# Batch 0 of an attention and MLP kernel: weight decoding moved ahead of the gate product in VectorE's queue, value loads moved ahead, raw down words in another pool

## The chip, the cores and the metric

One core of a Trainium2 chip runs the whole program. The metric is the device time in microseconds, the median of several runs; lower is better. TensorE is called PE, VectorE DVE, ScalarE ACT, GpSimd POOL and SyncE SP, as in the profile.

## The reference, cut to what matters

```python
def _attn_ref(q, k, v, p):              # batch 8, 8 heads, seq 576, head_dim 64, 32 packed queries
    p_packed = sm_attn(p, k, v)         # softmax attention of the 32 packed queries
    return sm_attn(q, p_packed, p_packed)

x = attn_out.transpose(0, 2, 1, 3).reshape(4608, 512)
g = x @ w_gate                          # [512, 1536]
x = (silu(g) * (x @ w_val)) @ w_out     # first MLP, d_ff 1536
h = x @ w_in                            # [512, 2048]
out = (h * cos(h)) @ w_out2             # second MLP, d_ff 2048
```

The weights come as 64-bit words, and the kernel makes 32-bit floats of them on the chip: this is the decoding that the change moves.

## The kernel before, in words

The order of the instructions on every engine is the order of the code (a manual schedule); each engine works through its own queue in order. Pools of buffers decide the rest: a new tile takes a free buffer, and its first writer waits until the last reader of the tile before is done. Pool "c" (`ct`) has 19 buffers, pool "w" (`wt`) 24, "m" (`mt`) 12, "s" (`ht`) 6, and PSUM has 8 banks.

Batches `b` 0 to 7 go through attention and the first MLP one after another; the second MLP follows for all tokens (L559 and L586). Inside a batch, `a_up` makes the 12 blocks `f` of 128 columns of the hidden layer, each in two halves `c` of 288 tokens: PE makes the gate `pg` and the value `pv`, ACT the silu, DVE the product `h` (L396), then ACT makes the rounded high part `g` (L77) and DVE the low part `g` (L78). This last pair is put off by one half: `flush_split` issues it in front of the next half's `h`. `a_down` multiplies by the down weights `wo` in 8 steps `n` (L438), and between these steps stands the attention of the next batch: `a_s1`, `a_t`, `a_pp`, `a_ppt`, `a_s2`, `a_wp`.

Batch 0 differs, for it also decodes the weights. There are 36 units of 128x512 words: 24 of gate and value weights (`wg`, two per block `f`) and 12 of down weights (`wo`, three per output block). A unit goes through three steps, and `u_step(k, n)` issues the next `n` units of step `k`:

- step 0, `u_load`: SP starts the DMA of the raw words (`raw`, 512 KB).
- step 1, `u_act`: ACT reads the words twice (L89 and L90) and leaves `dec` and a first version of the output.
- step 2, `u_dve`: DVE puts them together (L96 and L99). For a down unit, `flush_wo` then issues the split of the unit before into high (ACT L77) and low part (DVE L78).

Up to the loop over batches four units have been through step 2, six through step 1 and eight through step 0. From there `extra(0, f, c)` issues one of each at the end of each half. In block `f` PE first makes the first half of the sum of all four gate and value products (`u` = 0, L372), then `a_wp0(f + 1)` projects the decoded weights of the next block with the packed values (`wp`, L325: first with unit 2(f+1), then with unit 2(f+1)+1), then it makes the second half of the sums (`u` = 1). ACT copies the projection out of PSUM (`wpf`, L333) and then takes the silu of block `f`.

The value tiles `vt` of batch 1 are loaded by SP in `a_down(0)`, step 1; they take four buffers of pool "c", and `a_pp(1)` reads them in front of step 3. The raw words of the first eight down units are in pool "w", those of the last four in pool "c".

Of the kernel before, what the change touches and what calls it, by code (L numbers as in the profile page):

```python
# [19 lines left out]
B, H, S, D, NP = 8, 8, 576, 64, 32  # L20
NT, DM, DF1, DF2 = B * S, H * D, 1536, 2048
NF1, NF2, KD = DF1 // 128, DF2 // 128, DM // 128
NPAIR = H // 2
# [16 lines left out]
def attention_mlp_kernel(ctx: ExitStack, tc: tile.TileContext, qT, kT, vP, pP, wgv, w1o, w2, out):  # L40
# [15 lines left out]
    def ct(shape, dt, name):  # L56
        return sb.tile(shape, dt, tag="c", name=name, bufs=19)

    def mt(shape, dt, name):
        return sb.tile(shape, dt, tag="m", name=name, bufs=12)  # L60

    def ht(shape, dt, name):
        return sb.tile(shape, dt, tag="s", name=name, bufs=6)

    def bank(shape, name):
        return ps.tile(shape, F32, tag="b", name=name)
# [9 lines left out]
    def split(src, hi, lo, eng=DVE):  # L76
        ACT.activation(out=hi, in_=src, func=AF.Copy)  # L77
        eng.tensor_tensor(out=lo, in0=src, in1=hi.bitcast(F32), op=ALU.subtract)  # L78

    def raw_words(alloc, src, n):  # L80
        r = alloc([128, n, 2], U32, "raw")
        SP.dma_start(out=r, in_=src.bitcast(U32).rearrange("p (n t) -> p n t", t=2))
        return r
# [26 lines left out]
    def load_p(b):  # L110
        SP.dma_start(out=pt[b % 2], in_=pP[b])

    def load_k(b, j):
        kt[b, j] = mt([128, S], F32, "kt")
        SP.dma_start(out=kt[b, j], in_=kT[b, j])
# [5 lines left out]
    def load_v(b, j):  # L121
        vt[b, j] = ct([128, NC, 128], F32, "vt")
        SP.dma_start(out=vt[b, j], in_=vP[b, j])
# [132 lines left out]
    def u_load(n):  # L256
        if n >= len(units):
            return
        kind, a, i = units[n]
        d_raw[n] = raw_words(  # L260
            wt if 2 * NF1 <= n < 2 * NF1 + 8 else ct, wgv[a, :, 512 * i:512 * i + 512] if kind == "g" else w1o[a, i], 512
        )

    def u_act(n):
# [32 lines left out]
    def u_step(k, n):  # L297
        for _ in range(n):
            (u_load, u_act, u_dve)[k](u_next[k])
            u_next[k] += 1  # L300
# [3 lines left out]
    def w2_load(i):  # L304
        if i < 4 * NF2:
            w2_raw[i] = raw_words(mt, w2[i // 2, :, 256 * (i % 2):256 * (i % 2) + 256], 256)

    def w2_decode(i):
        w_ = ht([128, 256], F32, "w2f")
        t_ = ht([128, 256], F32, "w2t")  # L310
        decode_a(w2_raw[i], t_, w_)
        decode_b(w2_raw.pop(i), t_, w_)
        w2_out[i] = w_

    def w2_store(i):
        if i in w2_out:
            SP.dma_start(out=w2s[i // 2, :, 256 * (i % 2):256 * (i % 2) + 256], in_=w2_out.pop(i))
# [3 lines left out]
    def a_wp0(f):  # L321
        p_ = [bank([128, 256], "wp") for _ in range(2)]
        for c in range(4):
            for r in range(2):
                PE.matmul(  # L325
                    out=p_[r][cols(c), :],
                    lhsT=pp_of(0, r, c),
                    rhs=wg[f // 2, c // 2][rows(r), c % 2, f % 2, :],
                    start=True, stop=True,
                )  # L330
        wp[0, f] = ct([128, 2, 256], F32, "wpf")
        for r in range(2):
            ACT.activation(out=wp[0, f][:, r, :], in_=p_[r], func=AF.Copy)  # L333

    def a_wp(b, ms):
        p_ = {(m, r): bank([128, 2, 256], "wp") for m in ms for r in range(2)}
        for m in ms:
            for c in range(4):
                for r in range(2):
                    PE.matmul(  # L340
                        out=p_[m, r][cols(c)].rearrange("p a n -> p (a n)"),
                        lhsT=pp_of(b, r, c),
                        rhs=wg[m, c // 2][rows(r), c % 2].rearrange("p a n -> p (a n)"),
                        start=True, stop=True,
                    )
        for (m, r), p in p_.items():
            wp[b, m, r] = ct([128, 2, 2, 256], F32R, "wp")
            split(p, wp[b, m, r][:, 0], wp[b, m, r][:, 1])
# [3 lines left out]
    def flush_split():  # L352
        while pend_split:
            pend_split.pop(0)()

    def a_up(b):
        g = []
        for f in range(NF1):
            gt = ct([128, 2, S], F32R, "g")
            g.append(gt)  # L360
            if b > 0:
                if f in (2, 6):
                    a_wp(b, (f // 2 + 1, f // 2 + 2))
                w = [wp[b, f // 2, u][:, :, f % 2] for u in range(2)]
            else:
                w = wp.pop((0, f))
            banks = [(bank([128, HS], "pg"), bank([128, HS], "pv")) for _ in range(2)]
            if b == 0:
                for u in range(2):
                    for c in range(2):  # L370
                        for o, p_ in zip((0, 128), banks[c]):
                            PE.matmul(  # L372
                                out=p_, lhsT=w[:, u, o:o + 128], rhs=a2[u][:, HS * c:HS * c + HS],
                                start=(u == 0), stop=(u == 1),
                            )
                    if u == 0 and f + 1 < NF1:
                        a_wp0(f + 1)
            for c in range(2):
                sl = slice(HS * c, HS * c + HS)
                pg, pv = banks[c]  # L380
                for o, p_ in ((0, pg), (128, pv)):
                    n = 0
                    for u in range(2):
                        if b == 0:
                            continue
                        for (x, y) in PASSES:
                            PE.matmul(  # L387
                                out=p_, lhsT=w[u][:, x, o:o + 128], rhs=a2[u][:, y, sl],
                                start=(n == 0), stop=(n == 5),
                            )  # L390
                            n += 1
                s_ = ht([128, HS], F32, "silu")
                ACT.activation(out=s_, in_=pg, func=AF.Silu)  # L393
                flush_split()
                h_ = ht([128, HS], F32, "h")
                DVE.tensor_tensor(out=h_, in0=s_, in1=pv, op=ALU.mult)  # L396
                pend_split.append(lambda h_=h_, gt=gt, sl=sl: split(h_, gt[:, 0, sl], gt[:, 1, sl]))
                extra(b, f, c)
            prefetch(b, f)
        return g  # L400

    def extra(b, f, c):
        if b == 0:
            u_step(0, 1)
            u_step(1, 1)
            u_step(2, 1)
        elif b < B - 1:
            s_ = 24 * (b - 1) + 2 * f + c
            if s_ % 2 == 0 and s_ // 2 < 4 * NF2:
                w2_store(s_ // 2 - 1)  # L410
                w2_load(s_ // 2 + 1)
                w2_decode(s_ // 2)

    def prefetch(b, f):
        n = b + 1
        if n >= B:
            return
        if f == 4:
            load_p(n)
            for j in range(NPAIR):  # L420
                load_k(n, j)

    def a_down(b, g, steps):
        for n in range(8):
            for s_ in steps.get(n, ()):
                s_()
            if b + 1 < B and n == (1 if b == 0 else 0):
                for j in range(NPAIR):
                    load_v(b + 1, j)
            if b + 1 < B and n == (2 if b == 0 else 0):  # L430
                for j in range(NPAIR):
                    load_q(b + 1, j)
            o, c = n // 2, n % 2
            sl = slice(HS * c, HS * c + HS)
            acc = bank([128, HS], "o1")
            for f in range(NF1):
                for i, (x, y) in enumerate(PASSES):
                    PE.matmul(  # L438
                        out=acc, lhsT=wo[o, f // 4][:, x, f % 4, :], rhs=g[f][:, y, sl],
                        start=(f == 0 and i == 0), stop=(f == NF1 - 1 and i == 2),  # L440
                    )
            ev = ht([128, HS], F32, "x2e")
            ACT.activation(out=ev, in_=acc, func=AF.Copy)  # L443
            ACT.dma_start(out=x2d[o, :, S * b + HS * c:S * b + HS * c + HS], in_=ev)
# [37 lines left out]
    with tc.manual_schedule():  # L482
# [32 lines left out]
            u_step(1, 2)  # L515

        a_s2(0, while_exps)
        u_step(2, 2)
        u_step(1, 2)

        for b in range(B):
            g = a_up(b)
# [5 lines left out]
            n = b + 1  # L528
# [83 lines left out]
        for c in range(NCH + 3):  # L612
            t, f = divmod(c, NF2)
# [58 lines left out]
```

## Time and profile before

| | us |
|---|---|
| median of 3 runs | 1556.88 |
| the 3 runs | 1555.17 to 1558.46 |
| profiled execution, its own time | 1558.43 |
| profiled execution, span | 1556.6 |
| from 28.73 to 100.71: `a_up(0)` after its first projection | 71.98, PE busy 60.01 |
| from 100.71 to 155.33: `a_down(0)` | 54.62, PE busy 49.69 |
| from 155.33 to the end | 1401.27, PE busy 1394.13 |

The span is the time from the first to the last instruction; the execution's own time is 1.83 us more. The last three rows are stretches of the one profiled execution, with the time in which PE had a matmul at work in each; what is left in a stretch is time in which PE stood still.

### The profile page before, as it was taken

The numbers are of one execution on the slowest core, as the hardware profiler recorded it, in microseconds if no ns is written. First come the engines' busy times: TensorE is split into PE (matmuls) and PEld (weight loads), VectorE is DVE, ScalarE is ACT, GpSimd is POOL, SyncE is SP. The second block draws the span as 40 slices with busy tenths as digits, with TensorE's granted clock in tenths as the row PEclk, the third lists the DMA queues.
The fourth block names the chain that finished last, engine by engine and source line by source line (L and its number), as shares of the span: only waits on it lengthen the run. The fifth ranks groups of instructions, "written<-read, shape, count | busy, mean of one in ns | idle before, by whom it ended". The sixth has DMA issues, their size and how long they took to land.

```text
span 1556.6 us, 25488 instructions
## 1 busy us (share of the span) xinstructions
PE 1529.0 (98%) x10188; PEld 1317.6 (85%) x10188; DVE 983.6 (63%) x1888; ACT 713.1 (46%) x1454; POOL 3.0 (0%) x22
## 2 busy tenths in 40 slices
PE   8888999999999999999999999999999999999998
PEld 6568999989899998989888888888888888888887
DVE  5676737375573736354487676676766676766665
ACT  5674736456372735344453333433433433333333
POOL 0000000000000000000000000000000000000000
PEclk9999999999999999999999999999999999999999
DMA  8632433425151432320420101010100101010000
GB/s 313 206 132 72 138 105 111 136 63 173 49 170 54 135 111 72 104 74 17 125 80 1 55 1 55 0 55 0 36 19 1 55 1 55 0 55 0 27 1 28
DMA packets 63047, 112.28 MB, mean 72 GB/s; under 512 B 6992, under 2 KB 24656, under 8 KB 62928
## 3 DMA queue, kind: packets, MB, share of 16 engines
q1 hardware_dynamic: 53712, 101.21, 19.7%
q10 hardware_dynamic: 9216, 9.44, 1.7%
q8 instruction: 80, 1.31, 0.4%
q14 instruction: 39, 0.32, 0.1%
HBM read 83.36 MB, written 27.26 MB: 71 GB/s over the span
## 4 chain that ended last, share of the span: by engine, by line
PE 92%; DVE 4%; DMA 2%; ACT 2%; issue 1%; SPq 0%; ACTq 0%; DVEq 0%
PE acc L586 25%; PE h L559 25%; PE o L438 19%; PE pg L387 9%; PE pv L387 9%; PE wp L340 3%; DMA raw<-in_wgv 1%; DVE wg L96 1%; DVE wg L99 1%; DVE h L396 1%; DMA vt<-in_vP 1%; PE pp L194 1%; PE s L220 1%; PE wp L325 0%; DVE g L78 0%
## 5 line engine op out<-in xcount | busy, mean ns | idle before, releaser
L586 PE MATMUL acc<-wb,g 128*128 128x512 f32 x1728 | 417.0, 390 | 3.4 <-DVE g L78 2.8
L559 PE MATMUL h<-x,wb 128*128 128x512 f32 x1728 | 414.8, 389 | 0.0
L586 PEld LDWEIGHTS acc<-wb,g 128*128 128x128 f32 x1728 | 325.2, 188 | 72.2 <-DVE g L78 3.7
L559 PEld LDWEIGHTS h<-x,wb 128*128 128x128 f32 x1728 | 324.5, 188 | 67.2
L438 PEld LDWEIGHTS o<-g,wo 128*128 128x128 f32 x2304 | 308.9, 189 | 15.2 <-DVE d L241 5.9
L438 PE MATMUL o<-g,wo 128*128 128x288 f32 x2304 | 319.2, 298 | 1.3 <-DVE wo L78 1.0
L578 ACT ACTIVATE t<-t,half_pi 128x512 f32<-128x512 f32 x144 | 104.4, 725 | 272.5 <-DVE t L576 272.5
L571 ACT ACTIVATE t<-h,quarter 128x512 f32<-128x512 f32 x144 | 99.2, 689 | 198.2 <-PE h L559 198.0
L573 DVE TENSOR_SCALAR kk<-t 128x512 f32<-128x512 f32 x144 | 61.5, 427 | 192.9 <-ACT t L571 192.9
L387 PE MATMUL pg<-a,wp 128*128 128x288 f32 x1008 | 162.4, 296 | 0.0
L387 PE MATMUL pv<-a,wp 128*128 128x288 f32 x1008 | 160.6, 294 | 0.0
L387 PEld LDWEIGHTS pg<-a,wp 128*128 128x128 f32 x1008 | 142.4, 188 | 11.7 <-ACT wp L77 7.5
L387 PEld LDWEIGHTS pv<-a,wp 128*128 128x128 f32 x1008 | 143.0, 188 | 0.0
L78 DVE TENSOR_TENSOR g<-h,g 128x288 fp32r<-128x288 f32 x192 | 87.7, 457 | 86.2 <-ACT g L77 86.2
L579 DVE TENSOR_TENSOR t<-t,h 128x512 f32<-128x512 f32 x144 | 99.0, 688 | 28.0 <-ACT t L578 27.8
L393 ACT ACTIVATE silu<-pg 128x288 f32<-128x288 f32 x192 | 79.2, 412 | 78.0 <-PE pg L387 73.5
L575 DVE SCALAR_TENSOR_TENSOR t<-kk,t 128x512 f32<-128x512 f32 x144 | 99.7, 693 | 4.9
L574 DVE SCALAR_TENSOR_TENSOR t<-kk,h 128x512 f32<-128x512 f32 x144 | 99.1, 688 | 5.0
L78 DVE TENSOR_TENSOR g<-t,g 128x512 fp32r<-128x512 f32 x144 | 98.6, 685 | 0.7 <-ACT g L77 0.7
L396 DVE TENSOR_TENSOR h<-silu,pv 128x288 f32<-128x288 f32 x192 | 86.0, 448 | 19.2 <-ACT w2t L89 14.8
L443 ACT ACTIVATE x2e<-o 128x288 f32<-128x288 f32 x64 | 26.4, 413 | 146.4 <-PE o L438 146.4
L77 ACT ACTIVATE g<-t 128x512 fp32r<-128x512 f32 x144 | 89.7, 623 | 0.8 <-DVE t L579 0.8
(80 smaller groups left out, 1064.3 us busy)
## 6 DMA issues: line engine op xcount, KB each, us to landing
raw<-in_w SPq DMA_DIRECT2D x64, 256.0 KB, 2.9
raw<-in_wgv SPq DMA_DIRECT2D x24, 512.0 KB, 8.3
vt<-in_vP SPq DMA_DIRECT2D x32, 320.0 KB, 4.5
kt<-in_kT SPq DMA_DIRECT2D x32, 288.0 KB, 4.8
qt<-in_qT SPq DMA_DIRECT2D x32, 288.0 KB, 5.6
x2d<-x2e ACTq DMA_DIRECT2D x64, 144.0 KB, 1.8
x2r<-x2d SPq DMA_DIRECT2D x36, 256.0 KB, 3.9
out<-oe SPq DMA_DIRECT2D x35, 256.0 KB, 2.0
```

The lines of the kernel that those rows point to most:

```text
L77: ACT.activation(out=hi, in_=src, func=AF.Copy)
L78: eng.tensor_tensor(out=lo, in0=src, in1=hi.bitcast(F32), op=ALU.subtract)
L387: PE.matmul(out=p_, lhsT=w[u][:, x, o:o + 128], rhs=a2[u][:, y, sl], start=(n == 0), stop=(n == 5),)
L396: DVE.tensor_tensor(out=h_, in0=s_, in1=pv, op=ALU.mult)
L438: PE.matmul(out=acc, lhsT=wo[o, f // 4][:, x, f % 4, :], rhs=g[f][:, y, sl], start=(f == 0 and i == 0), stop=(f == NF1 - 1 and i == 2),)
L559: PE.matmul(out=p_, lhsT=wb["i", f][:, x, 128 * k:128 * k + 128], rhs=x2[t][k][:, y, :], start=(n == 0), stop=(n == 11),)
L571: ACT.activation(out=t_, in_=h_, func=AF.Identity, scale=1.0 / TWO_PI, bias=quarter)
L574: DVE.scalar_tensor_tensor(out=t_, in0=k_, scalar=-C_HI, in1=h_, op0=ALU.mult, op1=ALU.add)
L575: DVE.scalar_tensor_tensor(out=t_, in0=k_, scalar=-C_LO, in1=t_, op0=ALU.mult, op1=ALU.add)
L578: ACT.activation(out=t_, in_=t_, func=AF.Sin, bias=half_pi)
L579: DVE.tensor_tensor(out=t_, in0=t_, in1=h_, op=ALU.mult)
L586: PE.matmul(out=acc[t][i], lhsT=gt2[c][:, x, 128 * i:128 * i + 128], rhs=wb["o", f][:, y, :], start=(f == 0 and n == 0), stop=(f == NF2 - ...
```

## The change

Three things are changed, all of them in batch 0. The second step of the decoding is issued in front of each half's silu and product from block 1 on, no longer behind them, and five units instead of four are through it before the loop over the batches. The value tiles of batch 1 are loaded behind block 9 of `a_up(0)`, no longer in `a_down(0)`. All raw words of down units are in pool "w".

```diff
@@ u_load
         d_raw[n] = raw_words(
-            wt if 2 * NF1 <= n < 2 * NF1 + 8 else ct, wgv[a, :, 512 * i:512 * i + 512] if kind == "g" else w1o[a, i], 512
+            wt if kind == "o" else ct, wgv[a, :, 512 * i:512 * i + 512] if kind == "g" else w1o[a, i], 512
         )
@@ a_up, for each half c
+                if b == 0 and f > 0:
+                    u_step(2, 1)
                 s_ = ht([128, HS], F32, "silu")
                 ACT.activation(out=s_, in_=pg, func=AF.Silu)
                 flush_split()
@@ extra
         if b == 0:
             u_step(0, 1)
             u_step(1, 1)
-            u_step(2, 1)
+            if f == 0:
+                u_step(2, 1)
@@ prefetch
+        if f == 9 and b == 0:
+            for j in range(NPAIR):
+                load_v(n, j)
@@ a_down
-            if b + 1 < B and n == (1 if b == 0 else 0):
+            if 0 < b < B - 1 and n == 0:
                 for j in range(NPAIR):
                     load_v(b + 1, j)
@@ before the loop over the batches
         a_s2(0, while_exps)
-        u_step(2, 2)
         u_step(1, 2)
+        u_step(2, 3)
```

DVE's queue in `a_up(0)`, before: `h_537` is the product of block 2, first half, and `raw_433` holds unit 8.

```order
L396 TENSOR_TENSOR h_537<-silu_533,pv_509 128x288
L96 SCALAR_TENSOR_TENSOR wg_487<-dec_488,wg_487 128x2x256
L99 SCALAR_TENSOR_TENSOR wg_487<-raw_433,wg_487 128x2x256
L78 TENSOR_TENSOR g_507<-h_537,g_507 128x288
L396 TENSOR_TENSOR h_550<-silu_546,pv_511 128x288
L96 SCALAR_TENSOR_TENSOR wg_501<-dec_502,wg_501 128x2x256
```

The same place of the changed kernel: `h_487` is the product of block 1, first half, and `raw_435` holds unit 8.

```order
L398 TENSOR_TENSOR h_487<-silu_483,pv_457 128x288
L96 SCALAR_TENSOR_TENSOR wg_491<-dec_492,wg_491 128x2x256
L99 SCALAR_TENSOR_TENSOR wg_491<-raw_435,wg_491 128x2x256
L78 TENSOR_TENSOR g_455<-h_487,g_455 128x288
L398 TENSOR_TENSOR h_501<-silu_497,pv_459 128x288
L96 SCALAR_TENSOR_TENSOR wg_505<-dec_506,wg_505 128x2x256
```

The kinds of instruction follow each other as before; the unit that is decoded at a given place is two further on, so unit 8 has moved from behind a product of block 2 to behind the same product of block 1.

DVE's queue at the end of `a_up(0)`, before: `h_1031` is the last product of the batch, `raw_932` holds unit 27, `wo_1041` and `wo_1046` are the low parts of units 26 and 27, `mx` is the first step of the softmax of batch 1.

```order
L396 TENSOR_TENSOR h_1031<-silu_1027,pv_1001 128x288
L96 SCALAR_TENSOR_TENSOR wof_988<-dec_989,wof_988 128x512
L99 SCALAR_TENSOR_TENSOR wof_988<-raw_932,wof_988 128x512
L78 TENSOR_TENSOR wo_1041<-wof_974,wo_1041 128x512
L78 TENSOR_TENSOR g_997<-h_1031,g_997 128x288
L78 TENSOR_TENSOR wo_1046<-wof_988,wo_1046 128x512
L152 TENSOR_REDUCE mx_1071<-s1_1051 128x1
```

The same place of the changed kernel: `h_1032` and `h_1049` are the last two products, `raw_987` holds unit 28, `wo_1042` and `wo_1059` are the low parts of units 27 and 28.

```order
L96 SCALAR_TENSOR_TENSOR wof_1036<-dec_1037,wof_1036 128x512
L99 SCALAR_TENSOR_TENSOR wof_1036<-raw_987,wof_1036 128x512
L78 TENSOR_TENSOR wo_1042<-wof_1006,wo_1042 128x512
L78 TENSOR_TENSOR g_1010<-h_1032,g_1010 128x288
L398 TENSOR_TENSOR h_1049<-silu_1045,pv_1014 128x288
L78 TENSOR_TENSOR g_1010<-h_1049,g_1010 128x288
L78 TENSOR_TENSOR wo_1059<-wof_1036,wo_1059 128x512
L152 TENSOR_REDUCE mx_1084<-s1_1064 128x1
```

One unit more is decoded ahead of the softmax, and nothing of the decoding stands behind the last product any more but a low part.

SP's queue around the value loads, before: the raw words of down units 32 to 35 stand ahead of the four `vt` of batch 1.

```order
L82 DMA raw_1049<-in_w2 128x512
L82 DMA raw_1097<-in_w1o 128x1024
L82 DMA raw_1105<-in_w1o 128x1024
L82 DMA raw_1156<-in_w1o 128x1024
L82 DMA raw_1167<-in_w1o 128x1024
L123 DMA vt_1178<-in_vP 128x640
L123 DMA vt_1180<-in_vP 128x640
L123 DMA vt_1182<-in_vP 128x640
L123 DMA vt_1184<-in_vP 128x640
```

The same queue of the changed kernel: `raw_870` to `raw_936` are units 24 to 27, `raw_987` to `raw_1051` units 28 to 31.

```order
L82 DMA raw_870<-in_w1o 128x1024
L82 DMA raw_883<-in_w1o 128x1024
L82 DMA raw_922<-in_w1o 128x1024
L82 DMA raw_936<-in_w1o 128x1024
L123 DMA vt_942<-in_vP 128x640
L123 DMA vt_944<-in_vP 128x640
L123 DMA vt_946<-in_vP 128x640
L123 DMA vt_948<-in_vP 128x640
L82 DMA raw_987<-in_w1o 128x1024
L82 DMA raw_1004<-in_w1o 128x1024
L82 DMA raw_1034<-in_w1o 128x1024
L82 DMA raw_1051<-in_w1o 128x1024
```

The value loads have moved past eight loads of raw down words and one of the second MLP's, so four down units that stood ahead of them now stand behind.

## Rows read from the trace of the kernel before

**Rows 1.** The page, part 1: busy us, share of span, instructions.

```profile
PE 1529.0 (98%) x10188; PEld 1317.6 (85%) x10188; DVE 983.6 (63%) x1888; ACT 713.1 (46%) x1454; POOL 3.0 (0%) x22
```

**Rows 2.** Timeline of PE, 61 to 69: start, length, line, tiles, idle before.

```profile
61.84 0.64 PE L325 MATMUL wp<-wg,ppT 64*32 64x256 f32 x8 [1.18 <-DVE wg L99]
62.40 0.75 PE L372 MATMUL pg<-af,wpf 128*128 128x288 f32 x2
...
66.48 0.64 PE L325 MATMUL wp<-wg,ppT 64*32 64x256 f32 x8
68.29 0.64 PE L325 MATMUL wp<-wg,ppT 64*32 64x256 f32 x8 [1.18 <-DVE wg L99]
```

**Rows 3.** Groups by line, 36.63 to 94.69: count, busy, mean ns, idle before.

```profile
L325 PE MATMUL wp<-wg,ppT 64*32 64x256 f32 x148 | 11.8, 388 | 10.5 <-DVE wg L99 10.5
```

**Rows 4.** Timeline of DVE, the same period.

```profile
64.02 0.46 DVE L78 TENSOR_TENSOR g<-h,g 128x288 fp32r<-128x288 f32 x1 [2.24 <-ACT g L77]
64.40 0.45 DVE L396 TENSOR_TENSOR h<-silu,pv 128x288 f32<-128x288 f32 x1
...
67.55 0.69 DVE L99 SCALAR_TENSOR_TENSOR wg<-raw,wg 128x512 uint32<-128x512 uint32 x1
```

**Rows 5.** Timeline of ACT, the same period.

```profile
62.52 0.66 ACT L333 ACTIVATE wpf<-wp 128x256 f32<-128x256 f32 x2 [1.92 <-PE wp L325]
...
63.56 0.43 ACT L77 ACTIVATE g<-h 128x288 fp32r<-128x288 f32 x1
...
66.32 0.78 ACT L90 ACTIVATE wg<-raw,low 128x512 int32<-128x512 uint8 x1
```

**Rows 6.** Timeline of PE, `a_pp(1)` and step 3 of `a_down(0)`.

```profile
120.36 0.96 PE L194 MATMUL pp<-vt,ET 128*32 128x64 f32 x44 [0.61 <-ACT ET L185]
124.36 1.28 PE L194 MATMUL pp<-vt,ET 128*32 128x64 f32 x36 [3.04 <-DMA vt<-in_vP]
125.57 7.20 PE L438 MATMUL o<-g,wo 128*128 128x288 f32 x36
```

**Rows 7.** Timeline of SP's queue, 65 to 125.

```profile
68.68 4.35 SPq L82 DMA_DIRECT2D raw<-in_w1o  x8
...
104.46 17.31 SPq L123 DMA_DIRECT2D vt<-in_vP  x4
```

**Rows 8.** Windows: length; busy of PE, PEld, DVE, ACT, POOL; PEclk; DMA; GB/s.

```profile
123.50:130.40 6.90, 6.04 (x56) 5.87 (x57) 6.36 (x12) 2.72 (x5) 0.00 (x0) 0.51 0.71 230
132.60:155.33 22.73, 22.73 (x213) 20.37 (x212) 14.37 (x25) 8.68 (x17) 0.00 (x0) 1.00 0.08 27
774.83:780.00 5.17, 4.99 (x15) 3.96 (x16) 4.76 (x9) 3.10 (x7) 0.00 (x0) 0.67 0.41 106
```

**Rows 9.** Timeline of PE, the second projection inside the loop.

```profile
36.06 0.64 PE L325 MATMUL wp<-wg,ppT 64*32 64x256 f32 x8 [0.59 <-DVE wg L99]
```

**Rows 10.** Timeline of ACT: the last projection's copy out of PSUM.

```profile
94.81 0.66 ACT L333 ACTIVATE wpf<-wp 128x256 f32<-128x256 f32 x2 [1.90 <-PE wp L325]
```

**Rows 11.** The page, part 6: issues, KB each, us to landing.

```profile
raw<-in_wgv SPq DMA_DIRECT2D x24, 512.0 KB, 8.3
```

**Rows 12.** Timeline of DVE, the end of `a_up(0)`.

```profile
99.12 0.69 DVE L96 SCALAR_TENSOR_TENSOR wof<-dec,wof 128x512 uint32<-128x512 uint32 x1
...
101.78 0.68 DVE L96 SCALAR_TENSOR_TENSOR wof<-dec,wof 128x512 uint32<-128x512 uint32 x1
...
107.35 0.81 DVE L152 TENSOR_REDUCE mx<-s 128x1 f32<-128x288 f32 x2
```

**Rows 13.** Timeline of ACT, `a_down(0)`: exponentials of batch 1, then their transposes.

```profile
109.78 0.50 ACT L162 ACTIVATE E<-s,nm 128x288 f32<-128x288 f32 x1
...
119.82 1.43 ACT L185 ACTIVATE ET<-tp 128x384 f32<-128x384 f32 x4 [0.40 <-ACT x2e L443]
```

**Rows 14.** Waits of PE, 97 to 157: total, times, longest.

```profile
PE o L438 <- DVE wo L78: 1.0, 2, 0.8
```

**Rows 15.** Timeline of PE, the start of the second MLP.

```profile
775.01 4.14 PE L586 MATMUL acc<-wb,g 128*128 128x512 f32 x10 [1.90 <-DVE g L78]
```

## The prediction

> **What bounds the kernel now.** I read the page's busy times first: PE is at work 98% of the span [rows 1], so time can only be won where PE stands still or runs at a lower clock. The stretches in the table above say where that is: 71.98 - 60.01 = 12.0 us in `a_up(0)`, 54.62 - 49.69 = 4.9 us in `a_down(0)`, and 7.1 us in the 1401 us behind them. The change touches the first two alone.
>
> In `a_up(0)` the timeline of PE shows one period per block. From one second half of a projection to the next it takes 68.29 - 61.84 = 6.45 us, and 1.18 us of that PE waits for DVE's last decoding instruction, L99 [rows 2]. The group of this line over nine periods (148 instructions, 16 to a projection) has 10.5 us of idle time, all put down to L99 [rows 3]. DVE is no more a full engine than PE: it stands still 2.24 us and then works without a pause from 64.02 to 68.24 [rows 4]. Before 64.02 it waits for ACT's high part `g`, which stands in ACT's queue behind the copy of the projection [rows 5]. So this is a ring: PE's second half of the projection from 61.84 to the copy at 62.52 (0.7), ACT's copy, silu and `g` to 63.99 (1.5), DVE's low part, product and decoding, twice over, to 68.24 (4.2), and again PE: 6.4 us. No engine is full in it. It closes because the unit that the projection needs is decoded by the same DVE queue behind a product that needs the copy of the projection before.
>
> In `a_down(0)` the timeline shows PE waiting 0.61 us for `ET` and then 3.04 us for the value tiles `vt` [rows 6]. SP issued these from 104.46 on, and its queue needed 17.31 us for the four [rows 7]. Soon the granted clock drops: 0.51 on average from 123.5 to 130.4 [rows 8], and the 36 matmuls behind the wait take 7.20 us [rows 6]. Of the time from 132.6 to 155.33 PE is busy all 22.73 us, so what comes earlier there moves the end by as much [rows 8].
>
> **The ring is opened.** Nothing is added or taken away on DVE, ACT or PE in the loop; only which unit stands at a place changes, and it is two units further on. The units of the next projection are now decoded in front of the first product of the block before it, and PE's projection waits, by the semaphores of the changed program, for a PSUM bank that the product of the block before leaves. That product ends at 64.85, 2.33 us after the copy's start [rows 4, 5]; PE asks for the bank 4.5 us after it (66.48 + 0.56 - 62.52) [rows 2, 5]. PE's own period is then 0.56 (second half of the projection, 61.84 to 62.40) + 4.08 (sums, 62.40 to 66.48) + 0.56 (first half, taken as long as the second) = 5.20 us [rows 2]. That saves 1.25 us in each of nine periods, 11.3 us; by the idle column it is 10.5. The first projection in the loop waited 0.59 us [rows 9], and unit 5 is ready in time for it now. Together 11.1 to 11.9 us.
>
> The new wait is that of a decoding for ACT's first step of the same unit, issued only one half before. ACT's last first step of a period ends at 67.10, 4.58 us after the copy's start [rows 5]. The decoding behind it (two instructions of 0.69, 1.4 us) ends at 5.98, and DVE is wanted for the low part again at 5.20 + 1.50 = 6.70 (64.02 - 62.52, a period later) [rows 4, 5]. So 0.7 us are to spare, and ACT's 4.58 us and DVE's 4.22 us of work fit into 5.20. What is queued behind the waiting decoding, low part and product, is held for at most these 0.7 us; PE's sums wait for a product only two blocks later.
>
> The raw words have to come faster. SP issued all eight down units of pool "w" from 68.68 on [rows 7], ACT reads the first of them after 88.4 (one period ahead of 94.81) [rows 10], and a load of 512 KB lands 8.3 us after issue [rows 11]. A lead of 20 us bears a loop that ends 12 us earlier, the more as buffers come free earlier too. I cost it at nothing; without this cover a period would be what one load per half allows.
>
> **The end of the loop.** From block 10 on the splits of down weights join in, and DVE needs 101.78 - 99.12 = 2.66 us for each half [rows 12]; PE is not the slowest there, before or after. Before, it took from the last copy at 94.81 [rows 10] to the softmax's `mx` at 107.35 [rows 12] 12.5 us. After, I count from the copy at about 82.9: 1.3 us of ACT (copy and high part of unit 24), four halves of 2.66, 0.4 for a first step that is late, 0.5 for the last product's way over ACT and back: `mx` at about 95.7, 12.8 us. Unit 28's low part is added ahead of `mx`, the decoding behind the last product is gone. `mx` is 11.1 to 11.7 us earlier; I take 11.4.
>
> **`a_down(0)`.** From the exponentials to `ET` ACT works through the same list as before, one unit further on: 119.82 - 109.78 = 10.0 us [rows 13]. `ET` is thus 11.4 us earlier, at about 108.4. PE comes to it sooner still: the 1.0 us of waiting for `wo` goes [rows 14], for five units instead of four are ready. So the 0.61 us wait for `ET` grows to some 2 to 3.3 us. This is no price of its own, since the end is counted from `ET`, but nothing is won by PE being early. The `vt` now are issued at about 68 to 74, when buffers of decoded gate units come free, and the wait of 3.04 us goes whole.
>
> **The clock.** What a stall of 2 to 3.3 us does to it is open. After the 3.04 us one PE ran 6.04 us of work at 0.51, a loss of 6.04 x 0.49 = 3.0 us; after one of 1.90 us at 775 [rows 15] the clock was 0.67 over 5.17 us, a loss of 1.7 us [rows 8]. So the fall may come again whole (nothing won), shorter (1.3 won) or not at all (3.0 won). The expected stall lies between these rows; I take the middle of the first two, 0.7.
>
> **The sum.** 11.4 + 3.0 + 0.7 = 15.1 us. The profiled execution would take 1558.43 - 15.1 = 1543.3 us by its own time; that execution lay 1.55 us above the median of the runs, so the median should come to 1556.88 - 15.1 = 1541.8 us. A difference of 0.2%, 3.1 us, is about what a measurement can tell from no change here.
>
> **The rivals.**
>
> - No fall of the clock: 17.4 us, 1539.5. For it speaks that PE has no wait in the 7 us ahead of the new stall, against it both rows of stalls.
> - DVE or ACT takes over in the loop. If the held decoding costs more than the 0.7 us that are to spare, by late words or by slower hand-overs, the period becomes about 5.6 us: nine times 0.85 and 0.6 are won, 8.3 us, with 3.0 from `vt` 11.3: 1545.6. [...]
> - The change doesn't do what it says: the period stays at 6.45 us because it is not the decoding that PE lacks but a PSUM bank. Then 3.0 us of `vt` are won and with a stall of only 0.61 us left the clock's 3.0: 6.0 us, 1550.9. For it: the gap repeats, always as long. Against it: all 10.5 us are put down to L99 [rows 3]. [...]
> - Slower: the `vt` loads stand in SP's queue ahead of the words of units 28 to 35, and if their buffers are late, these are late. Unit 28 is read at about 89; with 8.3 us to land it must be issued by 80.7. SP held until then costs nothing, later one for one, and from 80.7 + 15.1 + 3.1, about 99, the kernel is slower. For it: the queue has been held by these four for 17.31 us [rows 7]. Against it: from 68 that would end at 85.5 and cost 5 us, not 18, and the buffers now come from gate units instead of `a_down(0)`'s own tiles.
>
> **Chances.** Forecast (clock falls, short or long) 0.53; no fall 0.19; loop not at PE's floor 0.14; loop unchanged 0.06; SP's queue late 0.05, of which 0.04 make it slower; 0.03 that gains and losses cancel. The range reaches from the no-fall case with 2 us for the spread of the runs and the loop's upper bound, 1537.5, to the slower loop, 1546. Faster by over 0.2%: 0.92; within: 0.04; slower: 0.04.
>
> **What would show it.** Right: the idle time of L325 in `a_up(0)` near nothing and a period of 5.2 us; the last copy at about 83 and `mx` at 95.7; a wait of PE for `ET`, none for `vt`; `vt` issued before 75. Wrong: a wait of L325 for `h` or of PE for `wpf`; ACT waiting for `raw`; SP standing at `vt` beyond 80.

## The result, and the profile after

The changed kernel takes 1535.75 us (median of 4 runs, 1534.86 to 1538.11) where the kernel before, run beside it, takes 1557.67 us: a ratio of 0.9864 with a 95% interval of 0.9846 to 0.9882. That is 21.9 us less; 15.1 us were forecast, and the time lies 1.75 us below the range. The profiled execution has a span of 1533.0 us, 23.6 us shorter than that of before; 1.6 us of this is a fall of the clock at the start of the second MLP that this execution did not have (below).

Timeline of PE in `a_up(0)`, after; it answers to [rows 2].

```profile
62.33 0.66 PE L325 MATMUL wp<-wg,ppT 64*32 64x256 f32 x16
...
67.00 0.66 PE L325 MATMUL wp<-wg,ppT 64*32 64x256 f32 x16
...
82.95 1.20 PE L142 MATMUL s<-kt,pt 64*32 64x288 f32 x32
```

The two halves of a projection, 8 recorded matmuls each in [rows 2], have become one row of 16, which takes 0.66 us where 8 took 0.64. From 34.31 on no projection waits any more, and the period is 4.67 us, not 5.20. Two stretches of nine periods, of after and, as a view of the kernel before, of before (columns as in [rows 8]):

```profile
34.90:76.93 42.03, 42.03 (x297) 28.25 (x289) 38.03 (x73) 40.43 (x90) 0.15 (x1) 1.00 0.75 260
```

```profile
36.63:94.69 58.06, 47.51 (x292) 29.39 (x288) 37.31 (x72) 40.34 (x90) 0.30 (x2) 1.00 0.48 169
```

Nine periods fell from 58.06 to 42.03 us, by 16.0; 11.3 were forecast. PE has no idle time in them any more, and ACT is at work 40.43 of 42.03 us, 96%.

From the last copy to `ET`, rows of ACT, DVE and ACT that answer to [rows 10, 12, 13]:

```profile
77.09 0.66 ACT L333 ACTIVATE wpf<-wp 128x256 f32<-128x256 f32 x2
...
102.63 1.43 ACT L185 ACTIVATE ET<-tp 128x384 f32<-128x384 f32 x4 [0.40 <-ACT x2e L449]
```

```profile
89.88 0.82 DVE L152 TENSOR_REDUCE mx<-s 128x1 f32<-128x288 f32 x2
```

The copy is 17.7 us earlier than in [rows 10], `mx` 17.5, `ET` 17.2. Timelines of PE and of SP's queue behind the loop, to be held against [rows 6, 7]:

```profile
103.17 2.12 PE L194 MATMUL pp<-vt,ET 128*32 128x64 f32 x80 [3.16 <-ACT ET L185]
105.22 5.81 PE L444 MATMUL o<-g,wo 128*128 128x288 f32 x36
```

```profile
64.65 4.98 SPq L123 DMA_DIRECT2D vt<-in_vP  x4
```

The value tiles are issued at 64.65, SP's queue is past them at 69.6, and nobody waits for them. PE waits 3.16 us for `ET` instead, and the granted clock falls again, but half as much: 8.00 x 0.21 = 1.7 us of it are missing here, before 6.90 x 0.49 = 3.4 [rows 8].

```profile
103.00:111.00 8.00, 7.83 (x118) 7.66 (x119) 6.15 (x11) 5.48 (x12) 0.00 (x0) 0.79 0.58 195
```

From `a_s1`'s first matmul to the end of `a_down(0)` it is 133.57 - 82.95 = 50.6 us, before 54.62. Where the 23.6 us went, along the two timelines: 0.5 ahead of block 1 (its first projection starts at 28.43, before at 28.96; in ten other kernels below that start in this way it lies between 28.5 and 29.5, so this part need not come from the change), 1.2 at the first projection in the loop, 16.0 in nine periods, minus 0.5 up to `ET`, 3.0 for `vt`, 1.4 and 0.2 for the clock and the rest of `a_down(0)`, 1.8 in the 1400 us behind it, nearly all at the start of the second MLP.

### The profile page after: what moved, and what is told of

It is laid out like the page before. It is cut to its first block, busy times and chain, and to the rows that moved or that the text cites. A ratio compares the mean times of both kernels' runs of the same rounds, so it can differ in the third digit from the quotient of the medians.

```text
span 1533.0 us, 25476 instructions
## 1 busy us (share of the span) xinstructions
PE 1518.8 (99%) x10188; PEld 1313.5 (86%) x10188; DVE 983.9 (64%) x1888; ACT 712.5 (46%) x1454; POOL 3.0 (0%) x22
## 4 chain that ended last, share of the span: by engine, by line
PE 96%; DVE 2%; ACT 1%; issue 0%; ACTq 0%; DVEq 0%
PE acc L592 25%; PE h L565 25%; PE o L444 19%; PE pg L387 9%; PE pv L387 9%; PE wp L340 3%; PE pg L372 1%; PE pv L372 1%; PE pp L194 1%; PE s L220 1%; PE s L142 1%; PE wp L325 0%; PE tp L183 0%; PE wm L106 0%; ACT E L162 0%
```

## The experiments

The theory after the result: the ring is opened as forecast, and what was mis-sized is PE's own period. The rival theories: the loads give part of what is put down to the loop, or ACT and DVE set the new period. Ratios are to runs of the kernel before in the same session (medians 1558.11, 1555.43, 1556.11 and 1557.20 us in the four).

### Each part alone

`e1_ahead_only` has the new decoding order with the old loads; `e2_loads_only` has the new loads with the old order:

```diff
@@ e1_ahead_only
-            wt if kind == "o" else ct,
+            wt if 2 * NF1 <= n < 2 * NF1 + 8 else ct,
-        if f == 9 and b == 0:
-            for j in range(NPAIR):
-                load_v(n, j)
-            if 0 < b < B - 1 and n == 0:
+            if b + 1 < B and n == (1 if b == 0 else 0):
@@ e2_loads_only
-                if b == 0 and f > 0:
-                    u_step(2, 1)
-            if f == 0:
-                u_step(2, 1)
+            u_step(2, 1)
+        u_step(2, 2)
         u_step(1, 2)
-        u_step(2, 3)
```

> The changed kernel with its decoding order, but the value loads and the pool of the last four raw down words as in the kernel before. Theory (the decoding order gives about 17 us up to ET, the loads about 4.5 us behind it, and the two add up): the projections of a block still go as one group of 16, period 4.67 us; the softmax at about 89.9 us and ET at 102.6 us as in the changed kernel; PE waits again about 3 us for vt, which become free with the progress of the same loop; about 1540 us. Rival (the value loads are tied to something that does not move with the loop): vt still land at about 124 us, PE waits more than 15 us for them, and nearly nothing is left of the gain, 1553 us or more.

> The value loads and the pool of the changed kernel, with the decoding order of the kernel before. Theory: the loop keeps its period of 6.45 us with 1.18 us of waiting for L99, the wait for vt of 3.0 us is gone, and with it part of the clock's fall of up to 3.0 us: 3 to 6 us faster than before, 1552 to 1555 us. Rival (the value loads ahead of the words of units 28 to 35 make these late): DVE or ACT wait for raw words at the end of the loop, and the time is that of before or longer, 1557 us or more.

Measured: e1 1539.58 us, ratio 0.9882 (0.9868 to 0.9896); e2 1552.56 us, 0.9965 (0.9954 to 0.9977). Both times are as the theory has them, and both rivals fall; but PE waited 1.0 us for `vt` in e1, not about 3. PE's timeline of e1:

```profile
104.91 1.06 PE L194 MATMUL pp<-vt,ET 128*32 128x64 f32 x44 [3.18 <-ACT ET L185]
106.98 1.28 PE L194 MATMUL pp<-vt,ET 128*32 128x64 f32 x36 [1.01 <-DMA vt<-in_vP]
108.20 6.96 PE L441 MATMUL o<-g,wo 128*128 128x288 f32 x36
```

The old place of the value loads moved with the loop: SP issued them at 87.74, and PE waited 1.0 us for them behind 3.2 us for `ET`, then took 6.96 us for the 36 matmuls, 1.9 more than in e2. In e2 the ring stayed as it was, and behind a wait of only 0.61 us the 36 matmuls took 5.06 us:

```profile
94.89 0.64 PE L325 MATMUL wp<-wg,ppT 64*32 64x256 f32 x8 [1.17 <-DVE wg L99]
...
121.10 1.43 PE L194 MATMUL pp<-vt,ET 128*32 128x64 f32 x80 [0.61 <-ACT ET L185]
122.46 5.06 PE L441 MATMUL o<-g,wo 128*128 128x288 f32 x36
```

The two gains, 18.5 and 5.6 us, add up to 24.1 and not to 21.9. The 2.2 us between them are no more than the intervals leave open. The rows show 1.4 us of them: with both parts PE reaches `a_pp(1)` further ahead of `ET`, and what e2 wins behind `ET` is lost again in part (product with `vt` and 36 matmuls in 1.43 and 5.06 us there, in 2.12 and 5.81 here).

### Which part of the lead opens the ring

`e5_front_four` decodes in front of the product but has four units ready before the loop; `e6_behind_five` has five, but each unit behind the product:

```diff
@@ e5_front_four
-        u_step(2, 3)
+        u_step(2, 2)
@@ e6_behind_five
-                if b == 0 and f > 0:
-                    u_step(2, 1)
-            if f == 0:
-                u_step(2, 1)
+            u_step(2, 1)
```

> The changed kernel with its decoding in front of the product, but four units decoded before the loop, as before the change: a lead one unit shorter. Theory (what opens the ring is that the second unit of a projection no longer waits for the last product of the block before; one step further ahead is enough): that unit is now ready about 3.8 us after ACT's copy (1.5 to the low part, 0.8 for low part and product, 1.4 for decoding), and PE asks for it 3.96 us after the copy, so the period stays within 0.2 us of 4.67 and the time within 2 us of the changed kernel plus at most 1 us of waiting for wo, 1536 to 1538 us. Rival (all of the lead is needed): L325 waits for L99 in every block again, its two halves fall apart, the period is 5.2 us or more, and the time is 1541 us or more.

> The changed kernel, five units decoded before the loop, but each unit behind the product of its half, as before the change. The second unit of a projection then stands behind the first product of the block before, at the same place of the queue as in the run with four units. Theory (the lead counts, not the place in front of or behind a product as such): as that run, period within 0.2 us of 4.67, 1536 to 1538 us. Rival (the place in front is what counts): period 5.2 us or more, 1541 us or more.

Measured: 1535.77 us, 0.9868 (0.9854 to 0.9883), and 1537.69 us, 0.9880 (0.9865 to 0.9895). In both the projections go as 16 every 4.67 us, in e5 from the second one in the loop on (the first still waits 0.59 us). Half of the lead would have been enough for the loop, by either way. PE's waits in e5 (line, what it waits for, total, times, longest):

```profile
PE pp L194 <- ACT ET L185: 0.6, 1, 0.6
...
PE o L444 <- DVE wo L78: 0.4, 2, 0.2
PE o L444 <- ACT wo L77: 0.3, 1, 0.3
```

With four units PE is held in three small pieces by `wo` ahead of `a_pp(1)`; its wait for `ET` shrinks to 0.6 us, and the granted clock stays whole there (mean 1.00 from 85 to 134 us; the 36 matmuls take 5.06 us). `ET` itself comes at 102.91 us, in the changed kernel at 102.63, and the work behind it hangs on `ET`. `a_down(0)` ends at 132.41, 1.2 us ahead of the changed kernel, by the clock. The medians do not show this; in the profiled execution of e5 the clock fell at the start of the second MLP (mean 0.98 from 700 to 800 us), where that of the changed kernel kept it (1.00 from 753.0 to 755.6).

### What a projection costs PE

`e3_split_halves` sets the sums of a half `c` between the two halves of the projection; `a_wp0` gets the column groups as an argument:

```diff
-                    if u == 0 and f + 1 < NF1:
-                        a_wp0(f + 1)
+                        if u == 0 and f + 1 < NF1:
+                            a_wp0(f + 1, (2 * c, 2 * c + 1))
```

> The changed kernel, but PE makes each projection in two groups of 8 matmuls, with a pair of sums between them, instead of one group of 16; the same matmuls in all. Theory (a group of projection matmuls costs about 0.57 us whether it has 8 or 16 of them, because the next weights wait for its end): the period goes from 4.67 to about 5.2 us, and over 11 projections the kernel is 5 to 6 us slower than the changed one, about 1541 us, which is what the forecast had. Rival (the period of 4.67 us is set by ACT, busy 94% of the loop, or DVE, and PE's groups do not matter): within 1 us of the changed kernel, 1536 us.

Measured: 1545.52 us, 0.9924 (0.9911 to 0.9936), 9.8 us slower than the changed kernel, so more than expected. PE's timeline:

```profile
41.30 0.64 PE L329 MATMUL wp<-wg,ppT 64*32 64x256 f32 x8
41.87 0.75 PE L378 MATMUL pg<-af,wpf 128*128 128x288 f32 x2
42.46 0.65 PE L378 MATMUL pv<-af,wpf 128*128 128x288 f32 x2
43.04 0.64 PE L329 MATMUL wp<-wg,ppT 64*32 64x256 f32 x8
...
46.71 0.64 PE L329 MATMUL wp<-wg,ppT 64*32 64x256 f32 x8
```

The period is 46.71 - 41.30 = 5.41, 0.74 more than 4.67. Beside the 0.57 us from a group to the next row, the step into it takes 0.58 us and the first one out of it 0.59, where two sums follow each other in 0.49: a group that stands apart also pays 0.2 us at its edges. In the changed kernel the weight loads show 0.39 us of `issue` ahead of a group and 0.41 behind it, where the tiles change between 128x128 and 64x32; what the 0.2 us go into these rows do not show.

```profile
62.33 0.18 PEld L325 LDWEIGHTS wp<-wg,ppT 64*32 64x32 f32 x16 [0.39 <-issue]
62.92 0.30 PEld L372 LDWEIGHTS pg<-af,wpf 128*128 128x128 f32 x2 [0.41 <-issue]
```

Eleven times 0.74 is 8.1 us; the rest of the 9.8 is not settled, though the mean clock of the profiled execution is lower (0.996, that of the changed kernel 0.999). The rival falls: ACT and DVE had the same work, and the period grew with PE's groups.

`e10_twice_0123` and `e11_twice_0101` make every projection twice, in two orders of the column groups `cols(c)`:

```diff
@@ e10_twice_0123
-        for c in range(4):
+        for c in (0, 1, 2, 3, 0, 1, 2, 3):
@@ e11_twice_0101
-        for c in range(4):
+        for c in (0, 1, 0, 1, 2, 3, 2, 3):
```

> The changed kernel with every projection multiplied twice, column groups in the order 0 1 2 3 0 1 2 3 (32 recorded matmuls for 16; the second pass writes the same values). Theory (matmuls of different column groups run side by side, those of the same group one after the other: this is why 16 take 0.59 us and 8 take 0.57): as the 32 matmuls of L142, 1.13 us to the next row, the group takes 1.0 to 1.1 us, the period 5.1 to 5.2, the kernel 5 to 6 us slower than the changed one, about 1541 us. Rival (a group costs a fixed 0.57 us of filling and draining, its matmuls next to nothing): period under 4.8, 1536 to 1537 us.

> The same 32 matmuls as the run before, in the order 0 1 0 1 2 3 2 3. Theory (side by side by column group, issued in order): the second pass over 0 1 waits for the first, the first over 2 3 runs beside it, so there are three rounds in place of two: the group takes 1.4 to 1.6 us, the period is 5.5 to 5.7, 4 to 5 us slower than the other order, about 1545.5 us. Rival (the price is one per matmul or per group, whatever its columns): the same time as the other order within 1 us.

Measured: 1543.53 us, 0.9916 (0.9902 to 0.9929), and 1543.22 us, 0.9911 (0.9897 to 0.9924); the period is 5.10 and 5.13 us. Eleven times 0.43 is 4.7 of the 7.8 us over the changed kernel, and behind the wait for `ET` the 36 matmuls took longer than there (6.75 and 6.62 us; mean granted clock in e10 0.70 from 109 to 120 us). PE's rows of e10, then of e11:

```profile
46.72 1.09 PE L325 MATMUL wp<-wg,ppT 64*32 64x256 f32 x32
47.74 0.75 PE L372 MATMUL pg<-af,wpf 128*128 128x288 f32 x2
```

```profile
45.36 1.12 PE L325 MATMUL wp<-wg,ppT 64*32 64x256 f32 x32
46.41 0.75 PE L372 MATMUL pg<-af,wpf 128*128 128x288 f32 x2
```

To the next row 8 take 0.57 us, 16 take 0.59, 32 take 1.02. A fixed price of a group is thus refuted (16 more cost 0.43), and so is a price per matmul (the second 8 cost 0.02). What fits is the column groups: unit 2f fills groups 0 and 1, unit 2f + 1 groups 2 and 3, and the halves run side by side, while a second pass over the same groups does not. One rival is left by these three numbers: a floor of 0.57 us below which up to 16 matmuls cost nothing, and a price per matmul above it, whatever the columns. A row of e11 decides. Ahead of block 1 PE waits in front of each half of the projection, so the second half, 16 matmuls over groups 2 and 3 alone in the order 2 3 2 3, stands in a row of its own:

```profile
30.02 1.07 PE L325 MATMUL wp<-wg,ppT 64*32 64x256 f32 x16 [0.17 <-DVE wg L99]
31.02 0.75 PE L372 MATMUL pg<-af,wpf 128*128 128x288 f32 x2
```

They take 1.00 us to the next row, at a granted clock of 1.00 (mean from 28 to 37 us), where 16 over all four groups take 0.59. The number is the same; only the groups differ. The three rounds that I expected for the order 0 1 0 1 2 3 2 3 were wrong: the order costs 0.03 us. As 2 3 2 3 takes 1.00 us alone and all 32 take 1.05, it ran beside 0 1 0 1 almost from the start, although it stands behind it in the queue. What lets it start early stays open.

Left was the question why the end of a wait of 1.18 us gave 1.78 us in every period. `e13_late_half_first` is the kernel before, with the halves exchanged:

```diff
-        for c in range(4):
+        for c in (2, 3, 0, 1):
```

> The kernel before, with the two halves of each projection exchanged on PE: the half that needs the unit decoded last comes first, so that PE waits for L99 ahead of all 16 matmuls. Theory (16 matmuls take as long as 8, so the first half was free and hid 0.6 us of the wait): the idle time of L325 in front of L99 grows from 1.18 to about 1.8 us per block, the 16 then go as one group in 0.59 us, and the period stays 6.45 and the time that of before within 1.5 us. Rival (a half costs 0.57 us of its own wherever it stands): the first half now comes on top, the period is 7.0 us, and over ten blocks the kernel is 5 to 6 us slower than before, 1561 us or more.

Measured: 1560.73 us, 1.0020 (1.0011 to 1.0029). By the time alone this lies between the two expectations; the rows decide.

```profile
56.00 0.67 PE L325 MATMUL wp<-wg,ppT 64*32 64x256 f32 x16 [1.83 <-DVE wg L99]
...
62.59 0.67 PE L325 MATMUL wp<-wg,ppT 64*32 64x256 f32 x16 [1.84 <-DVE wg L99]
```

PE waits 1.84 us, then the 16 go as one group, and the period is 6.59 us, not 7.0. So in the kernel before the real wait was about 1.8 us: the first half, free when it goes with the second, ran during it and covered 0.6 us of it. The 3.5 us more are, by the rows of the profiled execution: 0.13 in each of ten periods, 0.4 in two periods with a lowered clock (0.75 from 69.2 to 76.0 in the first), and 1.7 from the last projection to `a_s1`, which took 8.30 us (95.92 to 104.22) in place of 6.59. There, too, the granted clock was down:

```profile
96.00:104.20 8.20, 8.20 (x40) 5.64 (x39) 4.63 (x9) 5.61 (x14) 0.00 (x0) 0.79 0.01 2
```

### The new wait for ET

`e4_et_early` puts the two units of step 1 behind `ET`; `e8_et_early_spread` puts one unit less ahead of `ppu`:

```diff
@@ e4_et_early
-                for i in range(4):
-                    steps[i] = steps.get(i, ()) + (lambda: u_step(0, 1), lambda: u_step(1, 1), lambda: u_step(2, 1)) * 2
+                for i, k in ((0, 2), (2, 3), (3, 3)):
+                    steps[i] = steps.get(i, ()) + (lambda: u_step(0, 1), lambda: u_step(1, 1), lambda: u_step(2, 1)) * k
@@ e8_et_early_spread, from e4
-                for i, k in ((0, 2), (2, 3), (3, 3)):
+                for i, k in ((0, 2), (2, 2), (3, 2), (4, 1)):
-                steps[4] = (flush_wo,) + steps[4]
+                steps[5] = (flush_wo,) + steps[5]
```

> The changed kernel, but the two decoding units of step 1 of a_down(0) are put off to steps 2 and 3, behind ET in ACT's queue. Theory (PE's wait of 3.16 us for ET is the list of decoding in front of it in ACT's queue): ET about 4 us earlier, the wait under 1 us, the granted clock stays whole, 2 to 4.5 us faster than the changed kernel, 1531 to 1534 us. Rival (the units put off are then late themselves): PE waits about as long for wo in front of step 4, and the time stays within 1 us of the changed kernel.

> The kernel with ET early, but with two decoding units each in steps 2 and 3 and one in step 4, in place of three and three, so that the scaling ppu stands behind one unit less in DVE's queue. Theory (PE's remaining wait of 0.96 us in front of step 4 is ppu behind three decoding units): the wait goes, about 1 us faster than with ET early, 1530.8 us. Rival (the last units come too late by that): PE waits for wo in front of step 6 or the transposes, and the time is within 0.5 us of that kernel or longer.

Measured: e4 1531.79 us, 0.9837 (0.9824 to 0.9849); e8 1533.88 us, 0.9855 (0.9838 to 0.9871). PE's timeline of e4:

```profile
100.51 1.32 PE L194 MATMUL pp<-vt,ET 128*32 128x64 f32 x80
101.76 5.06 PE L444 MATMUL o<-g,wo 128*128 128x288 f32 x36
107.78 0.58 PE L210 MATMUL ppt<-ident,ppu 128*128 128x128 f32 x2 [0.96 <-DVE ppu L201]
```

The wait for `ET` and the fall of the clock behind it are gone (mean 1.00 from 83.55 to 130.68 us), so ACT's list of decoding ahead of `ET` was the bound of this stretch. Of the versions here e4 has the shortest time (e12, below, is not to be told from it); its interval lies below that of the changed kernel and just touches it. In e8 the 0.96 us wait is gone as well, and its stretch from `a_s1` to the end of `a_down(0)` is 45.8 us against 47.1 in e4, but this does not show in its median, which is 2.1 us longer than that of e4. The profiled execution of e8 had a fall of the clock behind the wait ahead of block 1 and one at the start of the second MLP (means of 0.81 from 28 to 37 and 0.76 from 750 to 757), that of e4 had none (mean 1.000).

`e7_busy_wait` and `e9_busy_13` fill PE's wait with dummy matmuls, 24 and 13:

```diff
@@ e7_busy_wait
+                steps[3] = (lambda: keep_busy(24),) + steps[3]
@@ e9_busy_13
+                steps[3] = (lambda: keep_busy(13),) + steps[3]
```

> The changed kernel with 24 dummy matmuls on PE in front of the multiplication that waits for ET; by the 20 that take 2.50 us before the loop they fill about 3.0 of the 3.16 us wait. Theory (the wait is ACT's and does not change, but PE's stall is what the granted clock falls after): no fall behind ET, the product with vt 1.3 us in place of 2.12 and the 36 matmuls behind it 5.0 to 5.1 us in place of 5.81; 1.0 to 1.6 us faster than the changed kernel, about 1534.5 us. Rival (the fall has to do with something else): the same rows and the same time as the changed kernel.

> As the run with 24 dummy matmuls, but with 13, because 24 took 5.52 us and not 3.0 (0.23 us each): 13 fill 3.0 us of the wait of 3.16 us. Theory (the clock's fall follows PE's stall; filled, it costs nothing): the product with vt starts about 0.6 us behind ET as before, takes 1.3 us, the 36 matmuls behind it 5.06 us in place of 5.81; 1.3 to 1.6 us faster than the changed kernel, about 1534.4 us, where no other fall differs. Rival (the fall has another cause): rows and time as in the changed kernel.

Measured: e7 1538.81 us, 0.9890 (0.9871 to 0.9909), runs from 1536.19 to 1542.63. Each dummy is recorded as two matmuls (48 for the 24), so the row of 20 that the expectation went by was ten dummies; the 24 took 5.52 us, 2.4 us more than the wait. The clock stayed whole there (mean 1.00 from 85 to 134 us), and from `a_s1` to the end of `a_down(0)` it is 51.2 us, 0.6 more than in the changed kernel. The rest of the 3.1 us between the medians is not explained by this; the two intervals overlap. e9 1535.44 us, 0.9867 (0.9853 to 0.9880). PE's timeline of e9 (26 recorded matmuls for 13 dummies), and a window over it:

```profile
101.63 3.06 PE L106 MATMUL wm<-zero 128*128 128x128 f32 x26
104.98 1.42 PE L194 MATMUL pp<-vt,ET 128*32 128x64 f32 x80 [0.29 <-ACT ET L185]
106.34 5.06 PE L444 MATMUL o<-g,wo 128*128 128x288 f32 x36
```

```profile
104.90:111.40 6.50, 6.42 (x119) 6.27 (x119) 4.73 (x9) 5.39 (x12) 0.00 (x0) 1.00 0.67 229
```

With the stall filled the clock stays at 1.00, and the stretch from `a_s1` to the end of `a_down(0)` is 49.2 us where the changed kernel has 50.6. The rows are as the theory has them, but of the 1.4 us the median shows only 0.3: in the profiled execution the clock fell at two other places (means of 0.81 from 28 to 37 and 0.76 from 753 to 760).

`e12_et_early_busy` adds to e8 seven dummies ahead of the projection that waits 1.87 us before block 1:

```diff
+                    if u == 0 and f == 0:
+                        keep_busy(7)
```

> The kernel with ET early and the units spread, with 7 dummy matmuls (1.6 us) on PE in front of the projection that waits 1.87 us for L99 before block 1. Theory (the clock's fall behind this place, which some executions show and others don't, and which makes the next block 1.7 us longer, follows this wait): no fall near 42 us of the record, and the runs lie closer together, about 1531.5 us where the kernel without dummies had 1532 to 1535. Rival (the fall has nothing to do with this wait, or the dummies push the projection back): the same times or longer.

Measured: 1532.22 us, 0.9841 (0.9827 to 0.9854), runs from 1530.40 to 1533.54. In its profiled execution the period behind this place takes 4.64 us (30.15 to 34.79), where e8, with a fall, had 6.33; but its runs lie no closer together than those of e8. Whether these dummies help is not settled.

## Why the prediction was wrong

**The ring, right in its parts.** The gap closed because the unit that the projection needs is decoded earlier: e2, which keeps the old order, keeps the wait. That it also stands in front of the product is not needed for it: e6 leaves it behind, one unit ahead, and has the same period. DVE waits in front of L96 for ACT, as foreseen, 0.4 us in every second half, and PE never feels it. The raw words, costed at nothing, cost nothing: ACT has no wait for `raw` from 25 to 135 us.

**PE's own period, the step that failed.** "0.56 (first half, taken as long as the second)" added two halves that run side by side. The period is 4.67 us: 4.08 for the sums and 0.59 for the whole projection; that it is the column groups which let the halves go together is shown by 16 matmuls over two groups (1.00 us) against 16 over four (0.59). Nine times 0.53 is 4.8 of the 5.8 us by which the copy was earlier than forecast; the first projection in the loop gave 1.2 instead of 0.6 for the same reason, and 0.5 us was there before the loop. "By the idle column it is 10.5" failed in the same way: the column shows a wait only as far as no other matmul runs in it.

**The rival in which ACT or DVE take over** did not come about, but only just: the 0.7 us to spare were counted for a period of 5.20, and at 4.67 ACT is 96% busy.

**The end of the loop, right.** From the last copy to `mx` it takes 12.8 us, as worked out; from `mx` to `ET` 12.75, before 12.47.

**`a_down(0)`, right.** The wait for `vt` is gone, PE's waits for `wo` too, and the one for `ET` is 3.16 us (2 to 3.3 forecast). The `vt` were issued at 64.65, a little ahead of the 68 to 74 forecast, as the loop is faster. e1 shows what their move is worth with the new loop: a 1.0 us wait and 1.2 us in the 36 matmuls behind it (6.96 against 5.81 us).

**The clock, between the cases.** The 36 matmuls behind the stall took 5.81 us; before 7.20 [rows 6], undisturbed 5.06. So 1.4 us were won where 0.7 were taken.

With the measured terms the sum reads 17.2 + 3.0 + 1.4 = 21.6 us, against 21.9 measured; 0.5 of the 17.2 lies ahead of block 1 and need not come from the change. The low end of the range reached only to the case without a fall of the clock; it took the loop's price as known.

## What to carry to other kernels

The idle time that a profile shows in front of a waiting instruction is not what the wait costs: what runs during it may be work that would be free later. Before pricing an engine's own period, look whether its pieces run side by side, here by the column groups in the code and by a row of the kernel before (L142, behind the loop), in which 32 matmuls take 1.20 us, less than the two rows of 8 in [rows 2] together (1.28):

```profile
100.71 1.20 PE L142 MATMUL s<-kt,pt 64*32 64x288 f32 x32
```

And when a stage gets shorter, follow the next engine's queue to its first consumer: 3.2 us of the gain stood in front of `ET`, and e4, with two decoding units put behind it, has neither that wait nor the fall of the clock.

## What the runs showed of the hardware

The granted clock falls at a place in one execution and not in another, although the waits ahead of it are the same, and all these places lie behind a wait of PE: that of 1.87 us ahead of block 1, that in front of `a_pp(1)` (3.04 us before, 3.16 after), that of 1.90 us at the start of the second MLP, and in e13 that of 1.8 us ahead of a projection, which has a fall behind it in some blocks and none in others (mean 1.00 from 62.6 to 69.1 us, 0.75 from 69.2 to 76.0). Ahead of block 1 the changed kernel and e6 have the same two waits; the window behind them, after and in e6:

```profile
28.00:35.00 7.00, 5.97 (x49) 3.58 (x49) 6.23 (x12) 5.37 (x12) 0.00 (x0) 1.00 0.73 281
```

```profile
28.00:37.00 9.00, 6.97 (x40) 4.18 (x48) 6.76 (x12) 6.37 (x13) 0.00 (x0) 0.81 0.59 214
```

The mean is 1.00 in the one (up to 37 us as well) and 0.81 in the other, and e6's next projection is 1.5 us later (6.11 us instead of 4.65 from one to the next). The second MLP's first ten matmuls behind its wait took 4.14 us before [rows 15], and after:

```profile
753.26 2.56 PE L592 MATMUL acc<-wb,g 128*128 128x512 f32 x10 [1.90 <-DVE g L78]
```

The wait is the same and the edit does not touch it; one execution lost 1.6 us there and the other nothing. Of the fifteen profiled executions (before, after and the thirteen experiments) ten took 3.93 to 4.63 us for these ten matmuls and five 2.55 to 2.60, all behind a wait of 1.90 or 1.91 us. The four runs of the changed kernel fit this: 1534.86 and 1534.95 us with a mean granted clock of 0.999, 1536.55 with 0.998, 1538.11 with 0.996. Differences of 1 to 2 us between two kernels can thus be a fall more or less.
